# Tile 2 of x turned by the crossbar instead of TensorE, and all slices of wk loaded over ScalarE's queue

## The chip, the cores and the metric

The kernel runs on one core of a Trainium2 chip. The metric is the device time of one execution in microseconds. A core has five instruction streams: TensorE (PE, matrix products), VectorE (DVE), ScalarE (ACT), GpSimd (POOL) and SyncE (SP), which computes nothing and here issues most of the DMAs. ScalarE and GpSimd issue DMAs too. All streams run on their own and meet at semaphores.

## What is computed

Input x has 2048 rows of 640. A gate g = sigmoid(x · gate_w) mixes two branches: linear attention (A) and an MLP with two layer norms and a shift of rows (B). Cut to what matters here:

```python
qkv = x @ wqkv                       # 640 -> 3 x 640
q, k, v = ...                        # 32 heads of 20
phi = lambda t: jnp.where(t > 0, t + 1, jnp.exp(t)) + 1e-6
pq, pk = phi(q), phi(k)
kv, z = einsum(pk, v), pk.sum(rows)
a = (pq @ kv / (pq . z)) @ wo
h = gelu(layernorm(x) @ w1); x1 = x + shift(h) @ w2
b = x1 + gelu(layernorm(x1) @ w3) @ w4
out = g * a + (1 - g) * b
```

The change lies wholly in the first products: x with the q part and the k part of wqkv, and the loads that feed them.

## The kernel before

The rows are cut into 16 tiles of 128. A product of TensorE contracts over the partitions, so x must be turned: `xT` holds x with its 640 columns on the partitions, in five slices of 128. The weights of q (`wq`) and of k (`wkg`) lie in five slices of 128 rows too. `wkg` has four columns more than wk: one of ones (so that the product gives row sums for the layer norm) and one with `gate_w` (so that it gives the gate's argument); the latter is made on TensorE from `gate_w` by a five-column product and copied into `wkg`.

**Queues.** The code writes one list of instructions for each engine, in program order, and computes the semaphore waits from what each reads and writes. An engine works its list in order, DMA issues too: a DMA that waits for something keeps everything behind it on that engine. `sch.dma("sp", ...)` puts a DMA on SyncE's queue, `"act"` on ScalarE's, `"pool"` on GpSimd's. `load_x`, `load_wq` and `load_wk` (from line 675) load one tile or one slice of 160 KB; `x_turn(t)` is a DMA from `x_tok` to `xT` that turns a whole tile in the crossbar. It waits for the tile's load.

The order of the first loads is written out by hand (lines 691 to 707). Before, SyncE issues x0, x1, wq2, x2, wk0, x3, wk2, wk4, x4, then the turn of tile 3, then one load of tiles 5 to 7, then the turns of tiles 4 to 7, one load of tiles 8 to 11, their turns, and so on. ScalarE issues wq0, wq1, wq3, wq4, wk1, wk3.

**TensorE's first work.** A warm-up of products whose result isn't used; `t_x(0)`, five transposes of x tile 0 through an identity matrix into PSUM, which VectorE copies to `xT`; then `q_three` (line 903): q of tiles 0, 1 and 2, slice by slice in an order written out by hand, with `t_x(1)` and `t_x(2)` in it as soon as their loads may have landed. In that list `(t, k)` is the product of tile t with slice k, `(t, None)` the transposes of tile t. `t_x(2)` also has the product for `gate_w`. Then come `k_two` (k of tiles 0 and 1, slice by slice, line 912), k of tile 2, and from there q and k of one tile after another: q(3), k(3), q(4), k(4), ... From tile 3 on `xT` comes from the crossbar.

`stream` (line 876) holds a pair of PSUM banks for every tile of such a list. `phi` (line 780) evacuates q or k: an Exp on ScalarE and two operations on VectorE. `k_out` adds the copy of row sum and gate and a sum of squares on ScalarE.

**The planner.** `_Items.run` puts all later items (layer norms, MLP, attention's products, outputs) in order by a simulated time with costs written in the code. Items of one stream stay in the order in which they were added; the first products are one stream, `A`.

Of the kernel before, what the change touches and what calls it, by code (L numbers as in the profile page):

```python
# [11 lines left out]
D = 640  # L12
# [3 lines left out]
NT = S // 128  # L16
NCH = S // 512
KD = D // 128
# [398 lines left out]
def _build(nc, A_x, A_wqkv, A_wo, B_w1, B_w2, B_w3, B_w4, gate_w, out, dbg=None, stop=None):  # L417
# [42 lines left out]
    ps = nc.alloc_psum_tensor("ps", [128, 8, 512], F32)  # L460
# [6 lines left out]
    ident = pa.alloc("ident", [128, 128], BF16)  # L467
# [19 lines left out]
    zb = pa.alloc("zb", [128, D], BF16)  # L487
# [9 lines left out]
    wkg = ra.alloc("wkg", [128, KD, NK], BF16)  # L497
# [17 lines left out]
    def bank():  # L515
        best = None
        for k_ in range(nbanks[0]):
            b = (bank_rr[0] + k_) % nbanks[0]
            if b in bank_pend or b in bank_hold:
                continue  # L520
            lk = sch.locks.get(b)
            tfree = 0.0 if lk is None else sch.ev_time.get((lk[1].sem, lk[1].val), 1e18)
            if best is None or tfree < best[0]:
                best = (tfree, b)
        bank_rr[0] = best[1] + 1
        bank_pend.add(best[1])
        return best[1]
# [30 lines left out]
    def nfree(ap):  # L558
        n = 1
        for d_ in ap.shape[1:]:  # L560
            n *= d_
        return n
# [23 lines left out]
    def pe(fn, reads, writes, cost=500.0):  # L586
        for w_ in writes:
            sp_, rl = sch.rects(w_)
            if sp_ == "ps":
                for (_p0, _p1, lo, hi) in rl:  # L590
                    for b in range(lo // PS_BANK, (hi - 1) // PS_BANK + 1):
                        bank_pend.discard(b)
        return sch.op("pe", fn, reads, writes, cost=cost)

    def mm_group(out_ap, pairs, reads_extra=()):
        n = len(pairs)

        def fn(e, out_ap=out_ap, pairs=pairs, n=n):
            ins = None
            for i, (l, r) in enumerate(pairs):  # L600
                ins = e.matmul(out_ap, l, r, start=(i == 0), stop=(i == n - 1))  # L601
            return ins
        reads = [a for p in pairs for a in p] + list(reads_extra)
        return pe(fn, reads, [out_ap], cost=n * (max(nfree(pairs[0][1]), 24) * 0.4167 + 2.5))
# [57 lines left out]
    def copy(engf, out_ap, in_ap):  # L662
        cost = None
        if engf is dve and in_ap.dtype == BF16 and out_ap.dtype == BF16:
            cost = 65.0 + nfree(out_ap) / 1.92
        return engf(lambda e: e.tensor_copy(out_ap, in_ap), [in_ap], [out_ap], cost=cost)
# [7 lines left out]
    def dma_in(out_ap, in_ap, key, **kw):  # L674
        return sch.dma("sp", out_ap, in_ap, key, **kw)

    def load_x(t):
        dma_in(x_tok[:, t, :], x2[128 * t:128 * (t + 1), :], "x%d" % t)

    def load_wq(k, queue):  # L680
        sch.dma(queue, wq[:, k, :], A_wqkv[128 * k:128 * (k + 1), 0:D], "wq%d" % k)

    def load_wk(k, queue):
        sch.dma(queue, wkg[:, k, 0:D], A_wqkv[128 * k:128 * (k + 1), D:2 * D], "wk%d" % k)

    def x_turn(t):
        sch.dma("sp", xT[:, :, 128 * t:128 * (t + 1)], x_tok[:, t, :], "trx%d" % (t % 4), transpose=True)

    gwr = xn[:, 1, 0:128]
# [2 lines left out]
    load_wq(0, "act")  # L692
    load_x(1)
    load_wq(1, "act")
    load_wq(2, "sp")
    load_wq(3, "act")
    load_x(2)
    load_wq(4, "act")
    load_wk(0, "sp")
    load_wk(1, "act")  # L700
    load_x(3)
    load_wk(3, "act")
    load_wk(2, "sp")
    load_wk(4, "sp")
    load_x(4)
    x_turn(3)
    sch.dma("pool", xn[0:KD, 1, 0:128], gate_w.rearrange("(k p) -> k p", p=128), "gw")
# [61 lines left out]
    WARM2 = 256  # L769

    def t_x(t):
        for k0, k1 in ((0, 1), (1, KD)) if t < 2 else ((0, KD),):
            b = bank()
            tr_group(b, [x_tok[:, t, 128 * k:128 * (k + 1)] for k in range(k0, k1)])
            if t == 2:
                mm_group(ps[:, b, 448:448 + KD], [(gwr, ident[:, 0:KD])])
            copy(dve, xT[:, k0:k1, 128 * t:128 * (t + 1)], psb(b, 0, 128 * (k1 - k0)).rearrange("p (k c) -> p k c", k=k1 - k0))
            if t == 2:
                copy(dve, wkg[:, :, D + 1:D + 2], ps[:, b, 448:448 + KD].rearrange("p (k o) -> p k o", o=1))

    def phi(b, dst, after_exp=None):
        se = slot("E", 3)
# [7 lines left out]
    def k_tile(t):  # L790
        tok = slice(128 * t, 128 * (t + 1))
        b = pair()
        mm_group(ps[:, b, 0:512], [(xT[:, k, tok], wkg[:, k, 0:512]) for k in range(KD)])
        mm_group(ps[:, b + 1, 0:130], [(xT[:, k, tok], wkg[:, k, 512:D + 2]) for k in range(KD)])
        k_out(t, b)
# [65 lines left out]
    def warmup(cols, cyc):  # L861
        b = bank()
        one = nc.const_aps.tensor(1.0, [128, 512], BF16)
        steps = [512] * (cols // 512) + [128] * (cols % 512 // 128)

        def fn(e):
            ins = None
            for n in steps:
                ins = e.matmul(ps[:, b, 0:n], one[:, 0:128], one[:, 0:n], start=True, stop=True)  # L869
            return ins  # L870
        pe(fn, [], [ps[:, b, :]], cost=cols * cyc)
# [8 lines left out]
    def stream(order, w, n2, done):  # L880
        bs = {}
        for t in sorted({t for t, k in order if k is not None}):
            bs[t] = pair()
            bank_hold.update((bs[t], bs[t] + 1))
        for t, k in order:
            if k is None:
                if t is None:
                    warmup(256, 0.42)
                else:
                    t_x(t)  # L890
                continue
            b = bs[t]
            l = xT[:, k, 128 * t:128 * (t + 1)]

            def fn(e, l=l, b=b, k=k):
                e.matmul(ps[:, b, 0:512], l, w[:, k, 0:512], start=(k == 0), stop=(k == KD - 1))  # L896
                return e.matmul(ps[:, b + 1, 0:n2], l, w[:, k, 512:512 + n2], start=(k == 0), stop=(k == KD - 1))  # L897
            pe(fn, [w[:, k, 0:512 + n2], l], [ps[:, b, 0:512], ps[:, b + 1, 0:n2]], cost=272.0)
            if k == KD - 1:
                bank_hold.difference_update((b, b + 1))  # L900
                done(t, b)

    def q_three():
        order = [(0, 0), (1, None), (0, 1), (1, 0), (1, 1), (0, 2), (1, 2), (2, None), (0, 3), (1, 3), (0, 4), (2, 0),
                 (2, 1), (1, 4), (2, 2), (2, 3), (2, 4)]
        stream(order, wq, 128, lambda t, b: phi(b, pq_tok[:, t + 1, :]))

    def k_out(t, b):
# [1 line left out]
        activation(junk[:, 0, :], x_tok[:, t, :], ACTF.Square, accum=st1[:, 1, t:t + 1])  # L910

    def k_two():
        stream([(0, 0), (0, 1), (0, 2), (1, 0), (0, 3), (1, 1), (1, 2), (0, 4), (1, 3), (1, 4)], wkg, 130, k_out)

    def addA(name, dur, fn, deps=()):
        IT.add("A", name, dur, fn, deps)
# [1 line left out]
    addA(("warm",), 0.0, lambda: warmup(WARM, 0.834))  # L918
    addA(("tx", 0), 0.28, lambda: t_x(0))
    addA(("warm", 1), 0.0, lambda: warmup(WARM2, 0.42))  # L920
    addA(("q", 2), 4.08, q_three)
    addA(("k", 1), 2.72, k_two)
    addA(("k", 2), 1.36, lambda: k_tile(2))
    for i in range(3, NT + 2):
        if i < NT:
            addA(("q", i), 1.36, lambda t=i: q_tile(t))
            addA(("k", i), 1.36, lambda t=i: k_tile(t))
        if i > 3:
            for t in range(3) if i == 4 else (i - 2,):
                addA(("g0", t), 0.27, lambda t=t: gt_tail(t), deps=[(("k", max(t, 1)), 2.0)])  # L930
# [280 lines left out]
    for c in range(NCH):  # L1211
        for j in range(KD):
            deps = [(("t1", u), 0.9) for u in range(4 * c, 4 * c + 4)] if j == 0 else []
# [6 lines left out]
    for t in range(NT):  # L1220
        c = t // 4
        deps = [(("w1", c, KD - 1), GEL)]
# [8 lines left out]
    for u in range(NT):  # L1231
        deps = [(("s2", u // 4), 3.2 + 0.9 * (u % 4))]
# [8 lines left out]
    for c in range(NCH):  # L1241
        for j in range(KFF):
            deps = []
# [4 lines left out]
            if j == 0:  # L1248
                deps = deps0 + [(("t2", u), 0.9) for u in range(4 * c, 4 * c + 4)]
# [9 lines left out]
                    IT.add("W3", ("w3h", c2), 1.27, lambda c2=c2: w3_half(c2), [(("t2", u), 0.9) for u in range(4 * c2 + 4, 4 * c2 + 8)])  # L1259
            IT.add("W3", ("w3", c, j), 1.08, lambda c=c, j=j: w3_group(c, j), deps)  # L1260
    for t in range(NT):
        deps = [(("zb",), 1.0), (("q", max(t, 2)), 2.0)]
        if t < 7:
            i = (5 * t) // 2 + 3
            deps.append((("w1", i // KD, i % KD), 0.0))
        else:
            i = 3 * (t - 7)
            if t >= 12:
                deps.append((("w4", t - 12), 0.0))
            if t < 12:  # L1270
                deps.append((("w3", i // KFF, i % KFF), 0.0))
        IT.add("QN", ("qs", t), 0.0, lambda t=t: qn_sum(t), deps)
        IT.add("QN", ("qn", t), 0.0, lambda t=t: qn_scale(t), [(("qs", t), 0.0)])
        IT.add("QT", ("qt", t), 0.0, lambda t=t: qt_tile(t), deps=[(("qn", t), 3.2), (("w2", NT - 1), 0.5), (("t2", 11 if t < 6 else NT - 1), 0.0)] + ([(("mt",), 0.0)] if t == 3 else []))
    for t in range(NT):
        c = t // 4
        deps = [(("qt", t), 3.0), (("w4load",), 0.0), (("m", 1), 1.0), (("mt",), 2.5)]
# [22 lines left out]
    order = IT.run(sch, hook)  # L1300
# [42 lines left out]
```

## Time and profile before

| | |
|---|---|
| Time, median of 7 executions | 260.81 us (259.8 to 261.72) |
| The profiled execution | 260.16 us, its span 258.9 us |
| TensorE's clock as granted | 1.00 throughout |
| Instructions | 4292 |
| Loads of 160 KB from x on SyncE | 5, median 5.1 us from issue to landing |
| Turns of x by the crossbar (`xT<-x_tok`) | 13, median 3.5 us to landing |
| First transposes on TensorE | start 3.74 us |
| First product of q / of k | 4.46 us / 10.13 us |

The span is the time from the first to the last instruction that the profile shows; the execution's own time is 1.3 us more. Lines of the profile name the engine, the line of the code (often that of a helper: L601 is the loop of `mm_group`, L896 and L897 the two products of `stream`, L612 the transposes, L869 the warm-up, L281 and L285 the DMA issues), what is written and read, and how often. Times in a timeline are microseconds from the span's start. The first products run at half the speed of later ones: 0.43 us for 512 columns until about 6.3 us, 0.22 us from 6.7 us on. A DMA's row shows the time that its engine spends to issue it; the time until its data has landed is a column of its own in the list of issues.

### The profile page before, as it was taken

The numbers are of one execution on the slowest core, as the hardware profiler recorded it, in microseconds if no ns is written. First come the engines' busy times: TensorE is split into PE (matmuls) and PEld (weight loads), VectorE is DVE, ScalarE is ACT, GpSimd is POOL, SyncE is SP. The second block draws the span as 40 slices with busy tenths as digits, with TensorE's granted clock in tenths as the row PEclk, the third lists the DMA queues.
The fourth block names the chain that finished last, engine by engine and source line by source line (L and its number), as shares of the span: only waits on it lengthen the run. The fifth ranks groups of instructions, "written<-read, shape, count | busy, mean of one in ns | idle before, by whom it ended". The sixth has DMA issues, their size and how long they took to land.

```text
span 258.9 us, 4292 instructions
## 1 busy us (share of the span) xinstructions
PE 256.1 (99%) x1684; PEld 132.7 (51%) x1684; DVE 152.1 (59%) x290; ACT 107.3 (41%) x217; POOL 94.0 (36%) x152
## 2 busy tenths in 40 slices
PE   8999999999999999999999999999999999999996
PEld 4555555544454554555445445554455544455453
DVE  2587877899914999999992407992033410143233
ACT  1396677751356866676853240005500045200000
POOL 5013995969952118767903202320011110021001
PEclk9999999999999999999999999999999999999999
DMA  6865986672764799552825650232000020000211
GB/s 199 232 154 147 206 192 119 181 126 50 100 126 81 123 405 285 66 103 51 104 60 112 124 71 0 48 90 67 0 3 0 3 101 0 0 3 1 104 51 51
DMA packets 52677, 25.48 MB, mean 98 GB/s; under 512 B 44037, under 2 KB 51246, under 8 KB 52657
## 3 DMA queue, kind: packets, MB, share of 16 engines
q1 hardware_dynamic: 50480, 20.82, 35.7%
q0 software_dynamic: 1168, 3.28, 5.5%
q10 hardware_dynamic: 1008, 1.11, 1.2%
q8 instruction: 13, 0.21, 0.4%
q14 instruction: 8, 0.06, 0.1%
HBM read 12.04 MB, written 2.62 MB: 57 GB/s over the span
## 4 chain that ended last, share of the span: by engine, by line
PE 99%; DVE 0%; issue 0%
PE ps L601 61%; PE ps L1182 22%; PE ps L803 8%; PE ps L896 2%; PE ps L869 1%; PE ps L1094 1%; PE ps L1164 1%; PE ps L897 1%; PE ps L612 1%; DVE x_tok L640 0%; PE ps L975 0%; PE ps L1004 0%; PE ps L1161 0%
## 5 line engine op out<-in xcount | busy, mean ns | idle before, releaser
L601 PE MATMUL ps<-xnT,w 128*128 128x512 bf16 x360 | 81.5, 379 | 0.0
L1182 PE MATMUL ps<-w,h2T 128*128 128x512 bf16 (+1 forms) x416 | 58.8, 299 | 0.0
L657 ACT ACTIVATE h2T<-ps 128x512 bf16<-128x512 f32 x52 | 30.5, 598 | 67.3 <-PE ps L601 67.3
L601 PEld LDWEIGHTS ps<-xnT,w 128*128 128x128 bf16 x360 | 34.2, 98 | 38.5 <-issue 0.7
L640 DVE SCALAR_TENSOR_TENSOR x_tok<-ps,stg,abx 128x512 bf16<-128x512 f32 (+1 forms) x32 | 17.3, 550 | 61.5 <-PE ps L1182 61.5
L623 POOL TENSOR_SCALAR abx<-x_tok,stg 128x640 f32<-128x640 bf16 x16 | 14.8, 925 | 99.8 <-DVE x_tok L640 94.9
L1182 PEld LDWEIGHTS ps<-w,h2T 128*128 128x128 bf16 x416 | 32.1, 98 | 24.9 <-issue 1.1
L623 POOL TENSOR_SCALAR xn<-x_tok,st 128x640 bf16<-128x640 bf16 x32 | 35.2, 1108 | 18.0 <-DMA xnT<-xn 17.6
L657 ACT ACTIVATE Er<-ps 128x640 bf16<-128x640 f32 x32 | 22.5, 708 | 15.2 <-PE ps L601 7.9
L656 ACT ACTIVATE junk<-x_tok 128x640 bf16<-128x640 bf16 x32 | 23.6, 739 | 3.4 <-DVE x_tok L638 2.8
L601 PE MATMUL ps<-M_sb,pqnT 128*128 128x512 bf16 (+1 forms) x160 | 24.4, 299 | 0.0
L657 ACT ACTIVATE hsT<-ps 128x512 bf16<-128x512 f32 (+1 forms) x32 | 19.0, 593 | 12.1 <-PE ps L601 11.6
L601 PE MATMUL ps<-w,hsT 128*128 128x512 bf16 (+1 forms) x160 | 23.7, 299 | 0.0
L640 DVE SCALAR_TENSOR_TENSOR abx<-ps,stg,abx 128x640 f32<-128x640 f32 x16 | 14.1, 883 | 15.8 <-PE ps L601 14.8
L601 PE MATMUL ps<-wkg,xT 128*128 128x130 bf16 (+1 forms) x140 | 21.4, 299 | 0.0
L601 PE MATMUL ps<-wq,xT 128*128 128x512 bf16 (+1 forms) x130 | 19.8, 299 | 0.0
L601 PEld LDWEIGHTS ps<-w,hsT 128*128 128x128 bf16 x160 | 13.3, 98 | 12.3
L601 PEld LDWEIGHTS ps<-M_sb,pqnT 128*128 128x128 bf16 x160 | 13.2, 98 | 10.8
L803 PE MATMUL ps<-pk_tok,x_tok 128*128 128x512 bf16 x80 | 17.8, 379 | 0.0
L623 DVE TENSOR_SCALAR Er<-Er 128x640 bf16<-128x640 bf16 x32 | 11.6, 363 | 8.1 <-ACT Er L657 8.0
L1123 DVE TENSOR_TENSOR pq_tok<-pq_tok,dnr 128x300 bf16<-128x300 bf16 (+1 forms) x48 | 15.7, 380 | 0.6
L638 DVE SCALAR_TENSOR_TENSOR x_tok<-ps,x_tok 128x640 bf16<-128x640 f32 x16 | 13.1, 820 | 4.4 <-PE ps L601 3.7
(78 smaller groups left out, 231.3 us busy)
## 6 DMA issues: line engine op xcount, KB each, us to landing
w<-in_B_w_dram SPq DMA_DIRECT2D x1, 2160.0 KB, 8.2
w<-in_B_w_dram SPq DMA_DIRECT2D x1, 2080.0 KB, 13.9
out_dram<-x_tok SPq DMA_DIRECT2D x3, 640.0 KB, 3.1
x_tok<-in_A_x_dram SPq DMA_DIRECT2D x2, 640.0 KB, 4.9
w<-in_B_w_dram POOLq DMA_DIRECT2D x8, 160.0 KB, 4.5
x_tok<-in_A_x_dram SPq DMA_DIRECT2D x5, 160.0 KB, 5.1
wv<-in_A_wqkv_dram POOLq DMA_DIRECT2D x1, 800.0 KB, 5.9
wq<-in_A_wqkv_dram ACTq DMA_DIRECT2D x4, 160.0 KB, 4.3
```

The lines of the kernel that those rows point to most:

```text
L601: ins = e.matmul(out_ap, l, r, start=(i == 0), stop=(i == n - 1))
L612: ins = e.transpose(o, s_, ident[:])
L623: return engf(lambda e: e.tensor_scalar(out_ap, in_ap, s1, s2, op0, op1), rd, [out_ap], cost=cost)
L638: return dve(lambda e: e.scalar_tensor_tensor(out_ap, in0, scalar, in1, op0, op1, accum_out=accum), rd, [out_ap, accum], cost=cost + 70.0)
L640: return dve(lambda e: e.scalar_tensor_tensor(out_ap, in0, scalar, in1, op0, op1), rd, [out_ap], cost=cost)
L656: return act(lambda e: e.activation(out_ap, in_ap, func, bias=bias, scale=scale, accum_out=accum), rd, wr, cost=cost)
L657: return act(lambda e: e.activation(out_ap, in_ap, func, bias=bias, scale=scale), rd, wr, cost=cost)
L803: ins = e.matmul(o, l, r, start=(t0 + q_ == 0), stop=(t0 + q_ == NT - 1))
L869: ins = e.matmul(ps[:, b, 0:n], one[:, 0:128], one[:, 0:n], start=True, stop=True)
L896: e.matmul(ps[:, b, 0:512], l, w[:, k, 0:512], start=(k == 0), stop=(k == KD - 1))
L1123: dve(lambda e, o=o, i0=i0, i1=i1: e.tensor_tensor(o, i0, i1, ALU.mult), [i0, dnr[:, 1, sd, :]], [o], cost=cost)
L1182: ins = e.matmul(o, l, r, start=False, stop=(i == KFF - 1), skip_group_check=(n0 > 0))
```

## The change

It does four things. TensorE no longer transposes x tile 2: a crossbar turn does, `x_turn(2)`, on SyncE. The load of x2 is third on SyncE's queue, and wq2 and wq3 change places between the queues. All five slices of wk leave over ScalarE's queue. The turn of tile 2 stands ahead of the loads of x3 and x4 on SyncE. In the order of products, q of tile 2 and k of tile 2 come after k of tiles 0 and 1, and the product for `gate_w` has a place of its own between q's slices (`gate_turn`).

```diff
     load_wq(0, "act")
     load_x(1)
     load_wq(1, "act")
-    load_wq(2, "sp")
-    load_wq(3, "act")
     load_x(2)
+    load_wq(2, "act")
+    load_wq(3, "sp")
     load_wq(4, "act")
-    load_wk(0, "sp")
-    load_wk(1, "act")
+    for k in range(KD):
+        load_wk(k, "act")
+    x_turn(2)
     load_x(3)
-    load_wk(3, "act")
-    load_wk(2, "sp")
-    load_wk(4, "sp")
     load_x(4)
     x_turn(3)
...
     def t_x(t):
-        for k0, k1 in ((0, 1), (1, KD)) if t < 2 else ((0, KD),):
+        for k0, k1 in ((0, 1), (1, KD)):
             b = bank()
             tr_group(b, [x_tok[:, t, 128 * k:128 * (k + 1)] for k in range(k0, k1)])
-            if t == 2:
-                mm_group(ps[:, b, 448:448 + KD], [(gwr, ident[:, 0:KD])])
             copy(dve, xT[:, k0:k1, 128 * t:128 * (t + 1)], ...)
-            if t == 2:
-                copy(dve, wkg[:, :, D + 1:D + 2], ps[:, b, 448:448 + KD].rearrange("p (k o) -> p k o", o=1))
+
+    def gate_turn():
+        b = bank()
+        mm_group(ps[:, b, 0:KD], [(gwr, ident[:, 0:KD])])
+        copy(dve, wkg[:, :, D + 1:D + 2], ps[:, b, 0:KD].rearrange("p (k o) -> p k o", o=1))
...
-    def q_three():
-        order = [(0, 0), (1, None), (0, 1), (1, 0), (1, 1), (0, 2), (1, 2), (2, None), (0, 3), (1, 3), (0, 4), (2, 0),
-                 (2, 1), (1, 4), (2, 2), (2, 3), (2, 4)]
+    def q_two():
+        order = [(0, 0), (1, None), (0, 1), (1, 0), (1, 1), (0, 2), (None, None), (1, 2), (0, 3), (0, 4), (1, 3), (1, 4)]
...
     def k_two():
-        stream([(0, 0), (0, 1), (0, 2), (1, 0), (0, 3), (1, 1), (1, 2), (0, 4), (1, 3), (1, 4)], wkg, 130, k_out)
+        stream([(0, 0), (1, 0), (0, 1), (1, 1), (0, 2), (1, 2), (0, 3), (0, 4), (1, 3), (1, 4)], wkg, 130, k_out)
...
-    addA(("q", 2), 4.08, q_three)
+    addA(("q", 1), 2.72, q_two)
     addA(("k", 1), 2.72, k_two)
-    addA(("k", 2), 1.36, lambda: k_tile(2))
-    for i in range(3, NT + 2):
+    for i in range(2, NT + 2):
```

In the new list `(None, None)` is `gate_turn`. One dependency of a later item, the normalizing of q, names the item of q(1) instead of q(2) for the first tiles.

## The prediction

> **What bounds the kernel now.** I read the page's busy shares first, then the chain of waits, then SyncE's own stretch of the timeline with the landings of its DMAs, and last TensorE's stretch to 21 us.
>
> ```profile
> PE 256.1 (99%) x1684; PEld 132.7 (51%) x1684; DVE 152.1 (59%) x290; ACT 107.3 (41%) x217; POOL 94.0 (36%) x152
> ...
> PE 99%; DVE 0%; issue 0%
> ```
>
> The chain that ended last is TensorE from end to end. Two things follow. TensorE work that goes away shortens the span one for one, and so does every new wait of TensorE lengthen it: there is no slack to swallow one. The chain in order of time shows the piece that the change touches:
>
> ```profile
> 7.00 0.21 PE ps L896
> 7.21 0.06 PE ps L897
> 7.27 0.22 PE ps L896
> 7.48 0.06 PE ps L897
> 7.54 0.28 PE ps L612 x5
> 7.82 0.01 PE ps L601
> 7.82 0.24 PE ps L896
> ```
>
> The five transposes of x tile 2 (L612) are 0.28 us of the chain; the gate product behind them (L601, five columns) is 0.01 us.
>
> What TensorE would wait for, if anything, are loads and turns on SyncE's queue:
>
> ```profile
> 3.13 0.43 SPq L285 DMA_DIRECT2D x_tok<-in_A_x_dram  x1
> 3.61 1.11 SPq L285 DMA_DIRECT2D wkg<-in_A_wqkv_dram  x2
> 4.76 0.64 SPq L285 DMA_DIRECT2D x_tok<-in_A_x_dram  x1
> 8.92 1.30 SPq L281 DMA_TRANSPOSE xT<-x_tok  x1
> 10.27 0.57 SPq L285 DMA_DIRECT2D x_tok<-in_A_x_dram  x1
> ```
>
> The loads of tiles 3 and 4 leave at 3.13 and 4.76; the turn of tile 3 stands until its load has landed (3.13 + 5.8 = 8.9), keeps SyncE 1.30 us, and only then does the load of tiles 5 to 7 (480 KB) leave. The next turn, tile 4, is issued at 10.88 and is slow for a reason that the issue lists of two narrow windows show (at 10.9 and at 17.5 us; the last column is us to landing):
>
> ```profile
> xT<-x_tok SPq DMA_TRANSPOSE x1, 4.3
> ...
> xT<-x_tok SPq DMA_TRANSPOSE x1, 2.5
> ```
>
> It took 4.3 us where an unobstructed one takes 2.5, because it lies behind the 480 KB in the same queue. So tile 4's turn lands at 10.88 + 4.3 = 15.2, which is 4.9 us after the 480 KB load's issue. TensorE asks for it here:
>
> ```profile
> 14.23 1.52 PE L601 MATMUL ps<-wq,xT 128*128 128x512 bf16 x10
> 15.59 1.53 PE L601 MATMUL ps<-wkg,xT 128*128 128x512 bf16 x10
> 16.95 1.52 PE L601 MATMUL ps<-wq,xT 128*128 128x512 bf16 x10
> ```
>
> These are q(3) at 14.23, k(3), and q(4) at 16.95. Tile 3's turn (8.92 + 2.5 = 11.4) is 2.8 us early, tile 4's 1.8 us. This 1.8 us is what the change spends.
>
> **What the Trainium skill says.** "DMA: Bandwidth & Descriptors", section "Issuing engines are not separate DMA queues": DMAs of SyncE and ScalarE run on the same 16 engines, so a second queue saves only issue time. The trace agrees: 380 GB/s from 7 to 8 us with both queues running. I give the move of wk no bandwidth. Same page, "Queues, rings and completion order": on each engine a queue's descriptors are taken in ring order; the 4.3 us above agrees. Same page, "Rules for kernel authors": a transpose next to ordinary DMAs needs no guard. Beside GpSimd's weight loads (25 to 28 us) turns land in 3.6 to 3.7 us instead of 2.5, so it costs time. "TensorE: Matmul & The Clock Gate", "Why this matters for your kernels": only idle gaps over some 3 us bring the slow clock back. The waits below are under 2 us; no wait in this trace tests it.
>
> **The change, part by part.**
>
> *TensorE's own work.* Minus 0.28 us (five transposes). The gate product stays. VectorE loses one 0.49 us copy, which is hidden. So everything from tile 0's k on is wanted earlier: the first k step 10.13 - 5 x 0.273 (tile 2's q steps, now later) - 0.28 = 8.49; q(2) 8.49 + 2.73 = 11.22; q(3) 13.95; q(4) 16.67.
>
> *The first weights.* Before, wq2 (third on SyncE) landed at 1.71 + 4.9 = 6.6, wq3 (third on ScalarE) at 1.73 + 5.1 = 6.85, x2 (fourth on SyncE) at 2.18 + 5.1 = 7.3, wq4 at 2.2 + 5.3 = 7.5. The bytes of each place in line are equal, so I keep the places: x2 6.6, wq2 6.85, wq3 7.3, wq4 7.5. Wanted: wq2 at 6.83, wq3 at 7.40, wq4 at 7.67. A wait of 0 to 0.1 us for wq2, nothing else. The margins are thin, but a wait here only moves TensorE towards the later turn and is not added to it.
>
> *wk on ScalarE.* Nine issues of 0.47 us end at 5.0 instead of 3.63; behind them is the table load (1.28 us), over by 6.3; the first Exp is wanted near 8. Hidden. When wq4 lands at 7.5 at most five slices of 164 KB are left: 0.43 us each at 380 GB/s, so wk0 by 7.95 and wk4 by 9.65; with tile 2's turn among them (about 0.9 us of the engines) wk4 by 10.55 at worst. Wanted at 8.49, 9.04, 9.58, 10.13 and 10.40. Cost 0, at worst 0.15. If this cover went, it would be the price of the last slice alone.
>
> *SyncE.* Its order is now x0, x1, x2, wq3, turn 2, x3, x4, turn 3, 480 KB, turn 4. Queued behind turn 2's wait is everything else of x. Step by step: x2 lands 6.6; turn 2 holds SyncE to 7.9 and lands at 9.1 (2.5) to 10.3 (3.7), wanted at 11.22, so hidden itself. x3 leaves at 7.95 instead of 3.13, x4 at 8.45. x3's flight is the value that I don't know: 2.9 is the first x load's own, and the 480 KB load, which also followed a turn, took 4.2, less 320 KB at 380 GB/s (0.84) is 3.4. I take 3.1: x3 lands at L = 11.05 (10.4 to 11.9 with x2 between 6.1 and 7.0 and a flight up to 3.5). Turn 3 from 11.05 to 12.35 lands at 13.55, wanted at 13.95: hidden by 0.4. The 480 KB leaves at 12.4 (10.27 before); turn 4 lands 4.9 later, at 17.3, wanted at 16.67. TensorE waits 0.63.
>
> *After that.* The 480 KB lands at 12.4 + 4.2 = 16.6, turn 5 at 19.1, and q(5) stands at 20.48 before; turns 6 and 7 follow 1.3 us apart, one pair of products every 2.7 or more. The 640 KB load leaves about 2.1 us later than its 18.62, so turn 8 lands near 27.5 for q(8) at about 29.5; tile 12's near 39 for about 41.4. All hidden. The order of later items hangs on ends relative to each other; I give it nothing.
>
> Sum: -0.28 + 0.63 = +0.35 us. Against the profiled execution 260.16 + 0.35 = 260.5; that execution lies 0.65 under the median 260.81, so the median comes to about 261.1. In general the shift is L + 6.26 - 16.95: nothing at L = 10.7, and never under -0.28.
>
> **The rivals.**
>
> *A, forecast (0.40): the cover of tile 4's turn is overspent by a little.* Shift 0 to +0.75, 261.1. For it: SyncE's order. Against: five terms added, each some tenths.
>
> *B (0.25): the cover holds.* x2 lands before 6.2 or the flight is 2.9 or less. L under 10.4, only the saving is left: 260.81 - 0.28 = 260.5. For it: TensorE asks later in executions slower at the start than the profiled one, while the DMAs don't. With a slow first stage, where transposes run at half speed (0.53 us for five at 5.20), the saving nears 0.5.
>
> *C, the other side (0.27): the same queue costs over a microsecond.* Turn 2 shares the engines with wk, x3 waits behind it in the ring: x2 6.9, flight 3.6, L = 11.85. Turn 3 then lands at 14.35, 0.4 late, turn 4 at 18.1: shift +1.16, 262.0. It decides from L = 11.5 on. For it: the 4.3 us of a turn behind a load, and 3.6 to 3.7 beside loads. Against: turn 2 is short, and wk has left the engines by about 9.7.
>
> *D (0.08): the weights bind.* With nine of the ten weight slices on one queue, TensorE stands at wq2 to wq4 or in the first k steps longer than the 0.6 us that turn 4 takes anyway, by 1 us: 261.8. Against: the landings above.
>
> **How the numbers follow.** About 0.3% (0.78 us) is what a measurement of this kernel can tell from no change. A gives 0.31 same, 0.07 slower, 0.02 faster. B gives 0.14 same and 0.11 faster, as the medians scatter by some tenths and the saving may near 0.5. C is slower, 0.27. D gives 0.04 slower and 0.04 same. Sums: faster 0.13, same 0.49, slower 0.38. The range from 260.2 (B, less scatter) to 262.1 (C) leaves about 2 in 10 out.
>
> **What would show it.** Five L612 transposes fewer, and q(3) reached some 0.28 us earlier; turn 2 issued near 6.6 and x3 near 8; x3 landed near 11; a gap on TensorE ahead of q(4), near 16.7, its releaser the DMA of xT; k steps without gaps. No gap there is B; gaps ahead of both q(3) and q(4) are C; gaps between 6.8 and 11 are D. I am wrong if TensorE's clock rises at another time, or if a gap appears after 21 us.

## The result, and the profile after

The changed kernel takes 261.88 us (median of 14 executions, 261.25 to 262.81) against 260.80 us of the kernel before (36 executions). The ratio is 1.0044, 95% interval 1.0029 to 1.0059: slower by some 1.1 us, clear of noise. The forecast was 261.1 us with a range of 260.2 to 262.1. The time lies in the range, at its slow end.

The page's busy shares and the summary of the chain that ended last, for the changed kernel (span 260.2 us, before 258.9):

```profile
PE 255.5 (98%) x1679; PEld 131.8 (51%) x1679; DVE 151.7 (58%) x289; ACT 107.3 (41%) x217; POOL 94.2 (36%) x152
...
PE 92%; DMA 5%; SPq 2%; DVE 0%; issue 0%
```

TensorE is busy 0.6 us less and has five products fewer. But the chain isn't TensorE's alone any more: 5% DMA and 2% SyncE's queue. They stand in one piece at the start. The same chain in order of time (start, length, what):

```profile
1.72 3.68 DMA x_tok<-in_A_x_dram
5.40 0.02 issue
5.42 1.31 SPq L281
6.73 0.05 issue
6.78 3.80 DMA x_tok<-in_A_x_dram
10.58 0.02 issue
10.60 1.20 SPq L281
11.80 0.04 issue
11.84 0.58 SPq L285
12.42 0.04 issue
12.47 5.74 DMA xT<-x_tok
18.20 0.05 issue
18.25 2.89 PE ps L601 x20
```

Read it from below. q(4) starts at 18.25 because the turn of tile 4 has just landed. That turn took 5.74 us from its issue at 12.47. Before it SyncE issued the 480 KB load (11.84), before that the turn of tile 3 (10.60), which waited for the load of x3 (6.78 to 10.58), which stood behind the turn of tile 2 (5.42), which waited for x2. This is the row of waits that the change built. TensorE's timeline shows what it costs (in brackets the idle time ahead and what ended it):

```profile
13.97 1.52 PE L601 MATMUL ps<-wq,xT 128*128 128x512 bf16 x10
15.33 1.53 PE L601 MATMUL ps<-wkg,xT 128*128 128x512 bf16 x10
18.25 1.53 PE L601 MATMUL ps<-wq,xT 128*128 128x512 bf16 x10 [1.40 <-DMA xT<-x_tok]
```

q(3) starts at 13.97, 0.26 us earlier than before. k(3) starts at 15.33, so q(4) could start 1.36 us later, at 16.69. It starts at 18.25. Minus 0.26, plus 1.56: that is the 1.3 us by which the two spans differ, and after q(4) the two chains are the same, piece by piece.

There is no second gap of that size. One small wait stands earlier: 0.46 us for wq2, which landed at 6.80. It isn't in the chain, for what TensorE loses there it would otherwise have waited ahead of q(4).

So far this is the forecast's mechanism at the forecast's place. Its size is not: 1.56 us instead of 0.63. And SyncE's chain was *earlier* than forecast. x3 landed at 10.58, not 11.05, the 480 KB load left at 11.84, not 12.4. By the forecast's own sum (L + 6.26) the turn of tile 4 was to land at 16.84. It landed at 18.2. The issue list of a narrow window around 12.7 us, where the last column is the time to landing:

```profile
xT<-x_tok SPq DMA_TRANSPOSE x1, 5.7
```

Before, the same turn behind the same load took 4.3 us. Where did nearly 1.5 us come from? The profile counts 16 DMA engines, and the trace has 16 landings for each of these DMAs; I take each as the landing of the part that one engine moves. The DMA has landed when its last part has. Times of parts, like all landings below, are counted from the profile's first instruction, as in the lines above:

```
part landed (us)     first    15th    last
before,  turn 4      14.86   15.03   15.15
changed, turn 4      16.53   16.67   18.20
changed, turn 3      12.85   12.96   12.97
```

Fifteen parts were there at 16.67, just in time for q(4) at 16.69. One was 1.53 us late. In the window from 16.0 to 17.2 us, the queues of the changed kernel (packets, MB, share of 16 engines' time):

```profile
q8 instruction: 1, 0.02, 4.9%
q1 hardware_dynamic: 55, 0.01, 4.7%
```

By the name of its kind, queue 8 brings instructions. Its one packet of 16 KB kept a DMA engine for 4.9% of 16 x 1.2 us, which is 0.94 us, from 16.16 to 17.11. A turn ends with 32 packets of 4 bytes, two for each part (turn 3, for one, has them from 12.46 to 12.61). Of turn 4's, 30 had run by 16.21, and the last two ran at 17.10, as the fetch ended. So theory S (SyncE's order makes the turn late) got a companion, F: an instruction fetch sits in front of the end of the turn on one engine. Two things are not shown. The trace names neither the DMA engine of a packet nor the engine whose instructions it brings; that the fetch and the late part share a DMA engine is inferred from the times, and that the instructions are TensorE's is an assumption of the expectations below. And the fetch covers only some 0.9 of the 1.53 us: the other parts landed 0.5 to 0.6 us after their last packets, the late one 1.1 us after its own. Where this further half microsecond comes from is open.

### The profile page after: what moved, and what is told of

Same layout as the page of the kernel before. It is cut to its first block, busy times and chain, and to the rows that moved or that the text cites. A ratio compares the mean times of both kernels' runs of the same rounds, so it can differ in the third digit from the quotient of the medians.

```text
span 260.2 us, 4285 instructions
## 1 busy us (share of the span) xinstructions
PE 255.5 (98%) x1679; PEld 131.8 (51%) x1679; DVE 151.7 (58%) x289; ACT 107.3 (41%) x217; POOL 94.2 (36%) x152
## 4 chain that ended last, share of the span: by engine, by line
PE 92%; DMA 5%; SPq 2%; DVE 0%; issue 0%
PE ps L601 59%; PE ps L1179 22%; PE ps L802 8%; DMA x_tok<-in_A_x_dram 3%; DMA xT<-x_tok 2%; SPq L281 1%; PE ps L1091 1%; PE ps L1161 1%; SPq L285 1%; DVE x_tok L640 0%; PE ps L972 0%; PE ps L1001 0%; PE ps L1158 0%
## 5 line engine op out<-in xcount | busy, mean ns | idle before, releaser
L640 DVE SCALAR_TENSOR_TENSOR x_tok<-ps,stg,abx 128x512 bf16<-128x512 f32 (+1 forms) x32 | 17.3, 550 | 61.5 <-PE ps L1179 61.5
L601 PE MATMUL ps<-wq,xT 128*128 128x128 bf16 (+1 forms) x140 | 21.3, 299 | 1.4 <-DMA xT<-x_tok 1.4
L623 DVE TENSOR_SCALAR Er<-Er 128x640 bf16<-128x640 bf16 x32 | 11.6, 363 | 10.4 <-ACT Er L657 10.3
L601 PEld LDWEIGHTS ps<-wq,xT 128*128 128x128 bf16 x140 | 11.3, 98 | 11.2 <-DMA xT<-x_tok 1.6
```

The costliest lines, as they stand in the source:

```text
L623: return engf(lambda e: e.tensor_scalar(out_ap, in_ap, s1, s2, op0, op1), rd, [out_ap], cost=cost)
L640: return dve(lambda e: e.scalar_tensor_tensor(out_ap, in0, scalar, in1, op0, op1), rd, [out_ap], cost=cost)
```

## The experiments

S is the forecast's mechanism. F is the fetch. W is the rival in which the weights bind, T that the late part was an accident of one execution. All ratios are to the kernel before, run on the same chip beside each.

**The changed kernel once more (e1).** No edit.

> The changed kernel a second time, for a second profile. Theory S (SyncE's order makes tile 4's turn late): a gap of TensorE ahead of q(4) of 1 us or more, ratio to before 1.003 to 1.006. Rival T (the gap came from one straggling part of that turn: 15 of its 16 parts had landed at 16.7 us, the last at 18.2): no straggler this time, the gap ahead of q(4) under 0.3 us in this profile. Rival W (weights): the wait for wq2 is 0.5 us or more and is kept to the end.

Ratio 1.0037 (1.0024 to 1.0050).

```profile
15.11 1.53 PE L601 MATMUL ps<-wkg,xT 128*128 128x512 bf16 x10
18.55 0.82 PE L601 MATMUL ps<-wq,xT 128*128 128x512 bf16 x3 [1.91 <-DMA xT<-x_tok]
```

The gap is there again, 1.9 us. Fifteen parts of turn 4 landed by 16.98, the last at 18.50; the fetch ran from 16.26 to 17.40. T falls. S by itself has a share here: q(4) could have started at 16.47 (15.11 + 1.36), so the fifteen parts too were 0.5 us late. W falls too: the wait for wq2 is 0.19 us here and the time no better.

**x3 and x4 loaded ahead of the turn of tile 2 (e2, and again as e11).**

```diff
-    x_turn(2)
     load_x(3)
     load_x(4)
+    x_turn(2)
     x_turn(3)
```

> The changed kernel with the loads of x3 and x4 ahead of the turn of tile 2 on SyncE's queue. S: x3 has landed before 9, the turn of tile 4 lands at 16 or earlier, no gap ahead of q(4), ratio to before 0.998 to 1.000. T: the straggler stays wherever the turn goes; with the turn 1.5 us earlier a gap of 0 to 0.5 us is left. W: nothing changes for the weights but that x3 and x4 share the engines with them, ratio stays at 1.004 or more.

> The changed kernel with x3 and x4 loaded ahead of the turn of tile 2, a second time: ratio to before 0.997 to 0.999, no gap of TensorE ahead of q(4), the fetch after the last part of tile 4's turn.

Ratios 0.9981 (0.9968 to 0.9993) and 0.9996 (0.9983 to 1.0009). In the first one's profile:

```profile
14.95 1.52 PE L601 MATMUL ps<-wkg,xT 128*128 128x512 bf16 x10
16.31 1.52 PE L601 MATMUL ps<-wq,xT 128*128 128x512 bf16 x10
```

q(4) follows k(3) without a gap; all parts of turn 4 landed by 14.10. Two lines changed places, and the whole loss is gone. The loss lies in SyncE's order, not in the crossbar turn of tile 2, not in ScalarE's queue. The second run doesn't confirm a gain over the kernel before: its interval holds 1.

**The turn of tile 4 ahead of the 480 KB load (e3).**

```diff
+        if c == 1:
+            x_turn(4)
         dma_in(x_tok[:, t0:4 * c + 4, :], ...)
-        for t in range(4 * c, 4 * c + 4):
+        for t in range(t0, 4 * c + 4):
             x_turn(t)
```

> The changed kernel with the turn of tile 4 ahead of the 480 KB load of tiles 5 to 7; all else stays. S: the turn of tile 4 is issued near 11.9 and lands near 14.5, no gap ahead of q(4); the 480 KB load leaves 1.2 us later, the turn of tile 5 lands near 20, wanted near 19.7 to 20.2, so a gap of up to 0.5 us there; ratio to before 0.999 to 1.002. W: ratio stays at 1.004 or more.

The ratio is 1.0074 (1.0061 to 1.0088), a clear miss of S's number. Turn 4 did land early, at 13.81, and q(4) had no gap. But TensorE waited further down, for the turns of tiles 8 and 12:

```profile
30.66 1.53 PE L601 MATMUL ps<-wq,xT 128*128 128x512 bf16 x10 [1.74 <-DMA xT<-x_tok]
43.54 1.53 PE L601 MATMUL ps<-wq,xT 128*128 128x512 bf16 x10 [0.74 <-DMA xT<-x_tok]
```

SyncE shows why:

```profile
12.63 0.58 SPq L285 DMA_DIRECT2D x_tok<-in_A_x_dram  x1
17.24 3.85 SPq L281 DMA_TRANSPOSE xT<-x_tok  x3
21.14 0.58 SPq L285 DMA_DIRECT2D x_tok<-in_A_x_dram  x1
25.52 5.22 SPq L281 DMA_TRANSPOSE xT<-x_tok  x4
```

The 480 KB load left at 12.63 instead of 11.84, and this time the late part was its own: fifteen parts at 16.25, the last at 17.23 (the fetch ran from 14.22 to 15.15, in the middle of this load). The turns of tiles 5 to 7 can't be issued before, the load of tiles 8 to 11 not before those, and so on. A delay in this row is handed on from load to load, until TensorE meets it. I had priced only the next link. The delay handed on is not the whole gap, though. Turn 8 was issued 1.0 us later than in the changed kernel (25.52 for 24.53), and it also took 5.1 us to land instead of 3.1. In e3 the first packets of GpSimd's weight loads ran while it was under way (from 26.67; 28.78 in the changed kernel, after turn 8 had landed). And TensorE, without its gap ahead of q(4), asked for tile 8 some 2 us earlier.

**All of wk on ScalarE's queue, alone (e4).** The kernel before with five `load_wk(k, "act")`, and SyncE's x loads moving up.

> The kernel before with one part of the change alone: all five slices of wk on ScalarE's queue (x3 and x4 leave SyncE earlier as a consequence, x2 is still turned by TensorE). S: the queue of wk costs nothing, ratio 0.998 to 1.001, no gap at all. W: nine slices of weights on one queue are late, TensorE waits in the first q or k steps, ratio 1.003 or more.

Ratio 0.9988 (0.9971 to 1.0005), no wait for wk. In this profile TensorE waited 0.8 us for x2 at 7.5 us, fourth on SyncE, so "no gap at all" was a miss. This part of the change costs nothing that can be measured.

**The queues of the change, TensorE as before (e8).** Order of loads as changed, the turn of tile 2 in it, but written to a place that nothing reads before it is overwritten; TensorE transposes tile 2 itself.

```diff
+    sch.dma("sp", xnT[:, :, 256:384], x_tok[:, 2, :], "trx2", transpose=True)
     load_x(3)
     load_x(4)
```

> The kernel before with the change's order on both queues, the turn of tile 2 included, but written to a place that nothing reads before it is overwritten; TensorE still transposes tile 2 itself and its order of products is that of before. S alone: the turn of tile 4 lands at 16.7 to 17.2 for q(4) at 16.95, gap 0 to 0.3 us, ratio 0.999 to 1.002. F: the 480 KB load and the turn lie 1.5 us later than before while TensorE's fetch stays, so the fetch falls among them, the last part is 1 us late or more, ratio 1.003 to 1.006.

Ratio 1.0053 (1.0036 to 1.0070).

```profile
18.14 1.04 PE L601 MATMUL ps<-wq,xT 128*128 128x512 bf16 x4 [0.98 <-DMA xT<-x_tok]
```

Fifteen parts of turn 4 had landed by 16.52, ahead of the 17.0 at which q(4) could start; the last landed at 18.09, and the fetch ran from 15.85 to 16.90. SyncE's order as I had priced it would have cost nothing in this execution. The late part cost all of the gap. The loss doesn't need the new order of TensorE's products.

**Moving the fetch (e5, e6, e9, with e7 and e10 as controls).** More, narrower products in the warm-up put more instructions ahead of everything. The comments in the diff tell the kernels apart, the numbers with a plus below are the instructions added.

```diff
-        steps = [512] * (cols // 512) + [128] * (cols % 512 // 128)
+        steps = [128] * (cols // 128)                                                   # e5, e7
+        steps = [256] * (cols // 256) + [128] * (cols % 256 // 128)                     # e6
+        steps = [512] * (cols // 512) + ([32] * 12 if cols > 512 else [128] * 2)        # e9, e10
```

> The changed kernel with the first warm-up in 27 products of 128 columns instead of 9 of up to 512: the same columns, 36 more instructions on TensorE ahead of everything. Theory F (TensorE's own instruction fetch, 16 KB on one DMA engine for 1 us, falls on the last part of tile 4's turn and makes it 1.5 us late): the fetch comes some 2 us earlier, all parts of the turn land together near 16.8, the gap ahead of q(4) is 0.3 us or less, ratio to before 0.998 to 1.001. Theory S alone (the turn is late because SyncE's order puts it late): gap 1.4 to 1.9 us as before, ratio 1.003 to 1.006.

> The changed kernel with the warm-up in products of 256 columns: 8 more instructions on TensorE, about as many as the change took away (10). F: the fetch comes 0.5 us earlier; if it is asked for while the 480 KB load still fills the engines, the straggler stays (ratio 1.003 to 1.006), if not it goes (1.001 or less). S alone: ratio 1.003 to 1.006.

> Control: the kernel before with the warm-up in 27 products of 128 columns. Both theories: ratio 0.999 to 1.001; were it faster by more, the gain of the changed kernel with the same edit would not be the fetch.

> The changed kernel with the last 384 columns of the first warm-up in 12 products of 32 instead of 3 of 128: 18 more instructions on TensorE, the wide products stay. F: the fetch is asked for 1.2 us earlier and falls before the 480 KB load fills the engines, all 16 parts of tile 4's turn land within 0.2 us of each other near 16.7, gap ahead of q(4) 0.5 us or less, ratio to before 0.999 to 1.002 unless another turn (tile 12's) is late. S alone: last part and gap as in the changed kernel, gap 1.4 us or more, ratio 1.003 to 1.006.

> Control: the kernel before with the same edit of the warm-up. F and S: no gap ahead of q(4), ratio 0.998 to 1.002. If it is slower by 1.003 or more, the edit itself costs time and is to be taken off the run beside it.

```
                        ratio (interval)             fetch          turn 4: 15th, last part   idle before q(4)
e5  changed, +36    1.0081 (1.0056 to 1.0107)    11.19 to 12.13        17.56   17.57             0.87
e6  changed, +8     1.0048 (1.0032 to 1.0065)    15.85 to 16.97        16.53   18.07             1.32
e9  changed, +18    1.0064 (1.0043 to 1.0084)    16.05 to 17.10        16.66   18.19             1.56
e7  before,  +36    1.0095 (1.0060 to 1.0131)    11.60 to 13.87        16.63   16.65             none
e10 before,  +18    1.0002 (0.9987 to 1.0016)    15.71 to 16.88        16.23   16.24             none
```

As times these failed as a test of F. The control e7 is itself slower, so e5's ratio says nothing of the changed kernel. In e7 the fetch fell into the first part of the 480 KB load, which took 5.8 us instead of 4.2, and the delay went down the row to tile 12 (2.4 us idle there, of which 1.6 us are a late part of turn 12 itself). And e9's 18 instructions did not move the fetch at all; the expectation that it would come 1.2 us earlier was wrong.

As traces they say more. Where the fetch came 5 us earlier (e5), all 16 parts of turn 4 landed within 0.15 us. A gap of 0.87 us was left, because turn 3 held SyncE for 2.0 us instead of 1.2 and the 480 KB load left at 12.60. (In that execution TensorE's granted clock fell to 0.96 between 20 and 60 us; only times before 20 us are used here.) Where it came at the end of turn 4 in the changed order (changed, e1, e6, e8, e9), one part was 1.5 us late, five times of five, and in each the last two packets of 4 bytes ran within 0.05 us of the fetch's end. It was not enough that the fetch came at that time: before, e2, e4, e10 and e11 have it there too, and no late part of more than 0.12 us. In e10 turn 4 landed at 16.24, close to the 16.67 of the changed kernel's fifteen parts, and whole. So lateness alone doesn't decide. One difference can be seen. In four of those five all 32 packets of 4 bytes had run no later than 0.04 us after the fetch began (before: by 14.57, with the fetch from 14.54). In the five late profiles even the other parts' packets still ran 0.05 to 0.24 us after it began. In e4 they ran until 0.26 us after it, though, and no part was late. So it is a matter of a quarter of a microsecond or less, and what decides whether the fetch gets in front is open.

The kernel before shows the same thing at another place. In its window from 26.5 to 27.9 us:

```profile
q14 instruction: 1, 0.01, 1.4%
```

This packet of 8 KB ran from 26.82 to 27.13. Fifteen parts of tile 9's turn had landed by 26.60, the last landed at 27.98, and its two packets of 4 bytes ran as that packet ended, at 27.13. In e2, e4 and e12 a part of tile 8's turn is late by 0.7 to 1.1 us in the same way. These speak for F. Not every late part has a fetch beside it: in e1 one of tile 10's turn came 1.4 us late without.

**The 480 KB load ahead of the turn of tile 3 (e12).** x3 and x4 stay behind the turn of tile 2.

```diff
     x_turn(2)
     load_x(3)
     load_x(4)
-    x_turn(3)
...
-        for t in range(4 * c, 4 * c + 4):
+        for t in range(4 * c - (c == 1), 4 * c + 4):
             x_turn(t)
```

> The changed kernel with the 480 KB load of tiles 5 to 7 issued ahead of the turn of tile 3 instead of behind it; x3 and x4 stay behind the turn of tile 2. S: the 480 KB load leaves near 8 instead of 11.9, the turn of tile 3 lands near 13 for q(3) at 13.9, the turn of tile 4 near 14.5, no gap ahead of q(4), ratio to before 0.998 to 1.001. F: if the fetch lands on the turn of tile 3 or 4 instead, its last part is 1.5 us late there and a gap of up to 1 us stands ahead of q(3). If the order of turn 2 ahead of x3 costs by itself, ratio 1.003 or more.

Ratio 0.9988 (0.9976 to 0.9999), 259.97 us against 260.26. SyncE's timeline from 10 to 18 us and, in a narrow window, turn 4 alone; then the issue list there, with the time to landing:

```profile
10.71 7.29 SPq L281 DMA_TRANSPOSE xT<-x_tok  x5
...
11.96 1.29 SPq L281 DMA_TRANSPOSE xT<-x_tok  x1
```

```profile
xT<-x_tok SPq DMA_TRANSPOSE x1, 2.5
```

x3's load left at 7.85 and turn 3 was issued at 10.71, as late as in the changed kernel. But the 480 KB load no longer waits for turn 3, and turn 4 doesn't lie behind it: 2.5 us instead of 5.7, landed at 14.5, no gap ahead of q(4). Turn 3 pays: it lay behind the 480 KB and landed at 13.91, just in time for q(3) at 14.02. The fetch (15.13 to 16.19) met turn 5: fifteen parts at 15.74, the last at 17.40, 1.66 us late. q(5) comes near 20, so nobody waits. The late part is still paid, at a place with room for it.

Here the interval ends just under 1. The forecast's saving of five transposes, 0.28 us, is a ratio of 0.9989. The three runs without a gap (0.9981, 0.9996, 0.9988) agree with it, but only two of the three intervals exclude 1, and e4, which keeps the five transposes, has the same 0.9988. That the saving reaches the end is not shown.

## Why the prediction was right, and where not

**What bounds the kernel, and where it would break.** Right: one gap, ahead of q(4), released by the DMA of xT, made by SyncE's order. e2 and e12 remove it by that order alone. q(3) was reached 0.26 us earlier (forecast 0.28), but this nearness is luck: the first products were faster than before, and a later start and the wait for wq2 took that back. In e1 q(3) came 0.48 us earlier.

**The step that failed** is "turn 4 lands 4.9 later, at 17.3". The 4.9 us between the issue of the 480 KB load and the landing of turn 4 was one measurement, from before. In the changed order it was 6.4 (11.84 to 18.2) and 6.5 in e1. The term missing in the sum is the late part, 1.5 us, at the instruction fetch. This is most of why the shift was about 1.1 us in the medians instead of 0.35.

**Luck.** That the time lies in the range owes something to luck. With the measured L the forecast's own sum gives 10.58 + 6.26 - 16.95 = -0.11 us, no loss at all. The fifteen parts that were not late show the same: against the moment at which q(4) could start they landed 0.5 us early in e8, within 0.2 us of it in the changed kernel, e6 and e9, and 0.5 us late in e1. The order by itself cost between nothing and half a microsecond; a term that the sum doesn't have made up the rest.

**A sign that was misread.** The kernel before had such a late part already, in tile 9's turn. The prediction took the "3.6 to 3.7 us" around it for the cost of running beside GpSimd's weight loads. These are medians of two turns each, and the first packets of those loads ran at 27.77, when all but the late part of tile 9's turn had landed. The turn's 3.9 us are the late part, 1.4 us on top of 2.5.

**Forecast A against rival C.** The size is C's (+1.16), the cause isn't. C was to decide from L = 11.5 on; L was 10.58, and 10.78 in e1. Turn 3 wasn't late.

**The terms of L.** Two errors cancelled. "I keep the places" was wrong for x2: third on SyncE, it landed at 5.40 (6.21 in e1), not 6.6; wq2 was slow in both places, 6.63 on SyncE before and 6.80 on ScalarE. x3's flight was 3.8 and 3.2 us, taken as 3.1. Turn 2 took 4.8 and 4.0 us, over the 3.7 that I gave as its upper end. It was under way together with the slices of wk, which landed until 9.6, and x3 landed only after it; rival C had named both.

**wk on ScalarE.** Right, nothing: wk4 landed at 9.6 for 10.4, and e4 measured it alone. **The wait for wq2.** 0.46 us instead of 0.1 at most, since TensorE's products were at full speed from 5 us in that execution and reached the slice earlier (before, they were at half speed until about 6.3 us). A rise of the clock at another time was one of the signs named for being wrong; here all that came of it is this wait. That such a wait isn't added to the later one was right.

**After that.** Right in the changed kernel: turn 8 landed at 27.6 (forecast 27.5), and no gap follows. The rest of the row is thin all the same: turn 12 landed at 37.8, but at 41.5 in e1, for a q(12) at 43.0. In e3, e5, e6 and e7 TensorE waited there, in e9 for tile 13.

**The chances.** A loss over 0.3% had 0.38, no change 0.49. The likelier case was the wrong one. A sum in which a landing time from one profile is carried to another order of queues deserved a heavier slow side.

## What to carry to other kernels

When an engine that issues DMAs waits for one landing before it issues the next load, price the whole row to its end, not the next link: the delay is handed on until a consumer meets it. Put loads, which wait for nothing, ahead of DMAs that wait; here the exchange of two lines was worth the whole loss. And where a deadline is met with less than 1.5 us to spare, look at the last of a DMA's parts, not at the usual one.

## What I had not expected of the hardware

- An instruction fetch of 16 KB keeps one DMA engine for 0.9 to 1.6 us in these traces (2.3 us once). A DMA whose last part ended with the fetch landed 1.5 to 1.7 us after its other parts in six profiles, 1.0 us where the fetch ran in the middle of a load (e3).
- The fetch isn't tied to a count of instructions in a simple way: 8 and 18 more on TensorE left it where it was, 36 more brought it 5 us earlier. In ten of the fourteen profiles it began within 0.3 us of the landing of the 480 KB load, but in e3 it ran in the middle of that load. What starts it was not tested.
- A turn of 160 KB took 2.4 to 2.6 us alone, and 3.8 to 4.8 us beside the five slices of wk on another queue (turn 2 in the eight profiles that issue it ahead of x3).
